# Where TensorE's small results stand in PSUM, and when a weight block's size is taken

## The chip, the cores and the metric

The kernel runs on one core of one Trainium2 chip. The time is the device time of one execution in microseconds (us). Five engines work side by side, each in the order of its own queue: TensorE (PE, matmuls and transposes; its weight loads are shown as PEld), VectorE (DVE), ScalarE (ACT), GpSimd (POOL), and SyncE (SP), which here only issues DMAs. Operands lie in SBUF, results of TensorE in PSUM, which has eight banks of 512 fp32 columns on each of 128 partitions.

## What is computed

Attention with a threshold, for 8 batches of 8 heads with 576 rows of 64, and behind it a feed-forward layer of 512 to 2048 to 512 with a softplus:

```python
scores = scale * np.matmul(q, k.transpose(0, 1, 3, 2))
thresh = np.max(scores, axis=-1, keepdims=True) - tau
scores = np.where(scores >= thresh, scores, -1000000000.0)
scores = scores - np.max(scores, axis=-1, keepdims=True)
attn = np.exp(scores)
attn = attn / (np.sum(attn, axis=-1, keepdims=True) + 1e-09)
attn_out = np.matmul(attn, v)
# (B, H, S, D) to (B * S, H * D), then
h = x @ w_in
g = np.maximum(h, 0.0) + np.log1p(np.exp(-np.abs(h)))
return g @ w_out
```

The weights `w_in` and `w_out` arrive as 64-bit floats. The kernel makes of each a scaled pair of fp16 numbers (a high and a low half), and its larger products are sums of three fp16 products.

## The kernel before

**Tiles and steps.** A unit is one batch and two heads; there are 32 units of 9 tiles of 128 score rows, 288 tiles in all. One pass of the main loop (line 1023) is a step and belongs to tile `g`. The letters of `PAT` (line 36) give the order in which a step issues its work: `R` the row maximum of tile g+2 (`row_max`, DVE, result `negm`), `e` its exponentials (`exps`, ACT, `e_all`, and then `thr`), `m` the mask of tile g+1 (`mask`, DVE, which reads the scores a second time), `h` and `l` the high and low fp16 halves of the weights (POOL, DVE), `T` transposes, `f` a share of the feed-forward matmuls, `p` a point, `S` the scores of tile g+3 (`scores`, PE), `x` the extras of the unit, a second `f`, `v` and `w` (`prep_w`, one block of weights in every second step), and a second `p`. So a step has two points.

**Points.** `defer(n, f)` (line 891) runs `f` at the nth point from now. A chain such as matmul, then copy, then use is spread over points in this way, so that no engine's queue has an instruction at its head whose input isn't there yet. From step 36 on (`TQ`), DVE, ACT and POOL each keep the order in which the program issues (class `Queue`, line 153; in the profile most lines of these engines are therefore L160). Before that, and on PE always, the framework orders instructions by priority and by its own estimate of when they are ready.

**PSUM.** Four of the eight banks are the scores': two buffers `banks[0]` and `banks[1]` (line 475), each of two banks, for the two halves of a tile's 576 columns. A half fills columns 0 to 287 of its bank. Tile n uses `banks[n % 2]`, so the scores of tile n+2 wait for the mask of tile n. The other four banks are a ring of four with the tag `g`. All other results of PE take their turns in it: the transposes of q and k (`tr`), those of the weights in the first five units (`tm`, `tr`; these units are "whole" and work in fp32), the products with v (`pv`), hidden layer (`h`, line 728) and output (`o`, line 792), and the small results that this change is about:
- `top_...` (line 193): one column spread over all partitions by a matmul, 128 columns, read by DVE; 8 times, one for each group of four weight blocks
- `topv` (line 384): the same for v, once in each unit
- `size_...` (line 292): four matmuls that sum a weight block over its columns, 4 columns, copied by ACT into `sums_w`; 32 times
- `rT` (line 629): the transpose of a unit's row sums, 9 partitions of 128 columns, read by ACT, once in each unit

**A block of weights.** `prep_w` (line 276) loads a block of 128 by 512 through `to_f32` (line 209). The 64-bit words are made into a 32-bit float in steps: `first` (ACT, the high word as a magnitude), `clamp` (POOL), and then `second` with n = 0, 1, 2 (DVE): the shift by three bits, the sign put in, and the low word's three bits put in. After the shift, one point on, `size` is taken. When the four blocks of a group are done, `over_all` finds the largest size, and `scaled` and `split` make the fp16 pairs. The blocks start in steps 0, 2, 4 and so on up to 62.

Of the kernel before, what the change touches and what calls it, by code (L numbers as in the profile page):

```python
# [25 lines left out]
P = 128  # L26
NG = 6
TB = 2
SB = 2
# [9 lines left out]
VO = (7, 8, 11, 12)  # L39
RT = 1  # L40
Q9 = (0.9, 1.1, 0.9, 1.1, 1.1, 0.8, 1.2, 0.6, 1.1)
WS2 = 2
LT = 4
WB = 3
NW = 33
# [21 lines left out]
def tile_kernel(ctx: ExitStack, tc: tile.TileContext, q, k, v, tau, w_in, w_out, out):  # L67
# [28 lines left out]
    ps_g = ctx.enter_context(tc.tile_pool(name="ps_g", bufs=GB, space=PSUM))  # L96

    nc.scalar.preload_act_table_set("exp_and_others")

    ones = apool.tile([P, S], F32, tag="R", bufs=1, name="ones")[:, 0:P]  # L100
    make_identity(nc, ones)
# [85 lines left out]
    def over_all(name, cols, then):  # L187

        col = cpool.tile([P, 1], F32, tag="col", bufs=3, name=f"col_{name}")
        vec.reduce_max(col, cols, axis=AX.X, apply_absolute_value=True)  # L190

        def spread():
            ps = ps_g.tile([P, 512], F32, tag="g", name=f"top_{name}")
            nc.tensor.matmul(ps[:, 0:P], col.to_broadcast([P, P]), ident, start=True, stop=True)
            defer(1, lambda: take(ps))

        def take(ps):
            top = cpool.tile([P, 1], F32, tag="top", bufs=3, name=f"top_{name}")
            vec.reduce_max(top, ps[:, 0:P], axis=AX.X)
            then(top)  # L200

        defer(1, spread)
# [6 lines left out]
    def to_f32(src, name, size, then, spare):  # L209

        while reading[0] >= WB or live[0] + 2 > NW:
            force()
        live[0] += 1
        if src.dtype == F32:
            m = piece([P, DM], F32, f"wa_{name}")
            nc.sync.dma_start(m, src)

            def magnitudes():
                a = wpool.tile([P, DM], F32, tag="wi", bufs=WB, name=f"wc_{name}")
                act.activation(a, m, AF.Abs)  # L220
                defer(1, lambda: size(a))
                defer(3, lambda: then(m))

            defer(WD, magnitudes)
            return
        reading[0] += 1
        words = wpool.tile([P, 2 * DM], U32, tag="wi", bufs=WB, name=f"wc_{name}")
        nc.sync.dma_start(words, src.bitcast(U32))
        words = words.rearrange("p (n t) -> p n t", t=2)
        low, high = words[:, :, 0], words[:, :, 1]  # L230

        def first():
            m = piece([P, DM], F32, f"wa_{name}")
            act.activation(m, high.bitcast(F32), AF.Abs, scale=2.0 ** 16)
            defer(1, lambda: clamp(m))

        def clamp(m):
            pool.tensor_scalar(out=m, in0=m, scalar1=W_MAX, scalar2=W_MIN, op0=ALU.min, op1=ALU.max)
            defer(1, lambda: second(m, 0))

        def second(m, n):
            mu = m.bitcast(U32)
            if n == 0:
                i = vec.tensor_scalar(out=mu, in0=mu, scalar1=3, scalar2=None, op0=ALU.logical_shift_left)
                defer(1, lambda: size(m))
            elif n == 1:
                to = piece([P, DM], F32, f"wb_{name}") if spare else m
                i = vec.scalar_tensor_tensor(out=to.bitcast(U32), in0=high, scalar=0x80000000, in1=mu,
                                                   op0=ALU.bitwise_and, op1=ALU.bitwise_or)
                m = to  # L250
            else:
                i = vec.scalar_tensor_tensor(out=mu, in0=low, scalar=29, in1=mu,
                                                   op0=ALU.logical_shift_right, op1=ALU.bitwise_or)
            behind(i, masked)
            if n < 2:
                defer(WS2, lambda: second(m, n + 1))
            else:
                reading[0] -= 1
                defer(1, lambda: then(m))

        defer(WD, first)
# [13 lines left out]

    def prep_w(kind, g, n):

        ms, tops = blocks.setdefault((kind, g), ([], []))
        late = WL.index((kind, g)) >= LATE

        wide = (w_in if kind == "i" else w_out).dtype != F32
        if n == 0:
            tops.append(cpool.tile([P, 16], F32, tag="sums_w", bufs=2, name=f"sums_{kind}{g}"))

        def got(m):
            ms.append(m)
            if n == 3:
                over_all(f"{kind}{g}", tops[0], scaled)

        def add(m):  # L290

            ps = ps_g.tile([P, 512], F32, tag="g", name=f"size_{kind}{g}_{n}")
            high = m.bitcast(BF16).rearrange("p (f t) -> p f t", t=2)[:, :, 1]
            for c in range(4):
                nc.tensor.matmul(ps[:, c:c + 1], high[:, c * P:(c + 1) * P], part, start=True, stop=True)
            defer(1, lambda: act.copy(tops[0][:, 4 * n:4 * n + 4], ps[:, 0:4]))

        def scaled(top):
            scale = cpool.tile([P, 1], F32, tag="wscale", bufs=2, name=f"wscale_{kind}{g}")
            to_scale(scale, top, 8)  # L300
            inverse(p_w[kind][:, g:g + 1], scale)
            for i in range(4):
                defer(2 * i, lambda i=i: split(i, scale))

        def split(i, scale):
            m = ms[i]
            w = piece([P, 2, DM], F16, f"w_{kind}{g}_{i}")
            if late:
                act.activation(w[:, 0, :], m, AF.Copy, scale=scale)
            act.activation(m, m, AF.Copy, scale=scale)  # L310
            defer(1, lambda: split_out(i, m, w))

        def split_out(i, m, w):
            if late:
                pool.tensor_tensor(out=w[:, 1, :], in0=m, in1=w[:, 0, :], op=ALU.subtract)
            else:
                halves(w[:, 0, :], w[:, 1, :], m)
            if kind == "i":
                wi[g, i] = w
            else:  # L320
                wo[4 * g + i] = w
            if i == 3:
                ready.add((kind, g))

        src = w_in[n * P:(n + 1) * P, g * 512:(g + 1) * 512] if kind == "i" else w_out[(4 * g + n) * P:(4 * g + n + 1) * P, :]
        to_f32(src, f"{kind}{g}_{n}", add, got, not late)


# [50 lines left out]
    def top_v(s):  # L379
# [1 line left out]
        vec.tensor_reduce(tops, s.vn.rearrange("p s d -> p (s d)"), axis=AX.X, op=ALU.max, apply_absolute_value=True)  # L381

        def spread():
            ps = ps_g.tile([P, 512], F32, tag="g", name=f"topv_{s.i}")
            nc.tensor.matmul(ps[:, 0:P], tops.to_broadcast([P, P]), ident, start=True, stop=True)
            defer(1, lambda: take(ps))

# [84 lines left out]


    e_all = cpool.tile([P, EB, S], F32, name="e_all")
    banks = [ps_s.tile([P, 2, 512], F32, tag="s", name=f"s_{i}") for i in range(SB)]
    nth = [0]

    def scores(s, t):
# [147 lines left out]
        vec.reciprocal(s.rs, s.rs)  # L626

    def row_scales_T(s):
        ps = ps_g.tile([P, 512], F32, tag="g", name=f"rT_{s.i}")
        nc.tensor.transpose(ps[0:9, 0:P], s.rs, ident)  # L630
        defer(1, lambda: row_scales_out(s, ps))

# [471 lines left out]
```

## Time and profile before

| | us |
|---|---|
| median of three runs | 1297.32 (1296.87 to 1297.4) |
| the profiled execution | 1296.41 |
| its span in the profile | 1294.6 |

The granted clock of TensorE was 0.996 of full speed on average. The profile's lines name an instruction group by its source line, engine, operation and the buffers it writes and reads (`out<-in`), then the count, the busy time, the mean duration in ns, and after the second bar the idle time of the engine just before, with what ended most of it (`<-`). The order of time (the timeline) has the start, the duration, the engine and line, and in square brackets the idle time before it. In the page's slices, each digit is the busy share of a fortieth of the span, in tenths:

```profile
PE   5999988888999999999999999999999999999998
PEld 4655544455565565665566656566657755554455
DVE  6889878988878987888778877786677666640111
ACT  5887887877877777777777787768676767644321
```

### The profile page before, as it was taken

The page shows a single profiled execution, that of the slowest core. Times are in us where ns is not written, and L with a number is a line of the kernel's source. Part 1 is how long each engine was busy: PE and PEld are TensorE (multiplying, and loading weights), DVE is VectorE, ACT ScalarE, POOL GpSimd, SP SyncE. Part 2 cuts the span into 40 slices and gives each one's busy share as a digit, 9 for nine tenths or more (in the row PEclk, how much of TensorE's full clock was granted, in tenths as well). Part 3 has the DMA queues.
Part 4 walks back from the last instruction along what each step waited for, and adds up shares of the span by engine and source line. Part 5 has one row for each costly group of instructions (what it writes and reads, how often), then busy time and mean ns, then how long its engine had stood idle before and what let it go on. Part 6 is the DMA issues. An engine that isn't in the chain of part 4 may idle for free.

```text
span 1294.6 us, 21819 instructions
## 1 busy us (share of the span) xinstructions
PE 1229.4 (95%) x7173; PEld 742.0 (57%) x7173; DVE 931.0 (72%) x1735; ACT 900.4 (70%) x1723; POOL 894.8 (69%) x970
## 2 busy tenths in 40 slices
PE   5999988888999999999999999999999999999998
PEld 4655544455565565665566656566657755554455
DVE  6889878988878987888778877786677666640111
ACT  5887887877877777777777787768676767644321
POOL 2465888888876787678777877787667777564332
PEclk9999989999999999999999999999999999999999
DMA  4545457756776777768766787776557555420010
GB/s 130 160 143 149 121 125 176 173 107 136 176 143 149 137 177 156 150 143 172 151 150 146 168 141 153 144 163 140 131 123 159 122 127 109 98 65 17 1 42 17
DMA packets 368738, 167.92 MB, mean 130 GB/s; under 512 B 320208, under 2 KB 346224, under 8 KB 368624
## 3 DMA queue, kind: packets, MB, share of 16 engines
q1 hardware_dynamic: 368624, 166.52, 58.1%
q8 instruction: 57, 0.93, 0.3%
q14 instruction: 57, 0.47, 0.1%
HBM read 56.62 MB, written 10.63 MB: 52 GB/s over the span
## 4 chain that ended last, share of the span: by engine, by line
PE 36%; ACT 16%; DVE 9%; POOL 8%; issue 7%; DMA 3%; SPq 0%; DVEq 0%; POOLq 0%; ACTq 0%
PE o L792 14%; PE h L728 12%; ACT st L160 5%; PE s L493 5%; ACT L160 5%; POOL g L160 4%; PE pv L608 3%; DVE h L160 3%; DVE e_all L160 2%; ACT e_all L160 2%; DVE negm L160 2%; POOL xl L160 1%; POOL h L160 1%; ACT q L160 1%; ACT kT L160 1%
## 5 line engine op out<-in xcount | busy, mean ns | idle before, releaser
L792 PE MATMUL o<-w_o,g 128*128 128x512 f16 x1728 | 405.0, 380 | 2.1 <-DVE xp L160 1.2
L728 PE MATMUL h<-xh,w_i 128*128 128x512 f16 (+1 forms) x1280 | 361.7, 359 | 5.9 <-ACT sums_i L160 3.6
L160 POOL TENSOR_SCALAR h<-e_all 128x576 f16<-128x576 f32 x243 | 228.9, 945 | 112.9 <-DVE e_all L160 110.4
L160 ACT ACTIVATE e_all<-s,negm 128x576 f32<-128x576 f32 x288 | 213.6, 742 | 119.1 <-DVE negm L160 113.1
L728 PEld LDWEIGHTS <-w_i 128*128 128x128 f16 x1920 | 179.0, 98 | 168.7 <-issue 13.2
L160 DVE SCALAR_TENSOR_TENSOR e_all<-s,thr,e_all 128x576 f32<-128x576 f32 x288 | 232.8, 808 | 53.9 <-ACT thr L160 53.1
L160 DVE TENSOR_REDUCE negm<-s 128x1 f32<-128x576 f32 x288 | 215.1, 747 | 69.6 <-PE s L493 68.2
L792 PEld LDWEIGHTS <-g 128*128 128x128 f16 x1728 | 159.2, 98 | 174.2 <-issue 3.5
L160 DVE SCALAR_TENSOR_TENSOR h<-e_all,h 128x576 f16<-128x576 f32 x243 | 236.5, 973 | 19.0 <-POOL h L160 18.5
L728 PE MATMUL h<-xl,w_i 128*128 128x512 f16 (+1 forms) x640 | 230.3, 360 | 1.2 <-POOL xl L160 1.1
L160 POOL TENSOR_SCALAR g<-st 128x512 f16<-128x512 f32 x144 | 97.7, 678 | 165.0 <-ACT st L160 160.2
L160 DVE SCALAR_TENSOR_TENSOR acc<-o,c,acc 128x512 f32<-128x512 f32 x108 | 80.1, 742 | 154.5 <-PE o L792 154.1
L160 POOL TENSOR_TENSOR g<-st,g 128x512 f16<-128x512 f32 x144 | 172.2, 1196 | 12.0
L493 PE MATMUL s<-kT,q 128*128 128x288 f32 x768 | 152.9, 327 | 15.5 <-DVE e_all L160 12.5
L160 ACT ACT_TABLE_LOAD x119 | 152.7, 1283 | 3.6 <-DVE negm L160 1.4
L160 ACT ACTIVATE st<-h,c 128x512 f32<-128x512 f32 x144 | 91.1, 683 | 79.6 <-PE h L728 78.8
L493 PEld LDWEIGHTS s<-kT,q 128*128 128x128 f32 x768 | 114.7, 191 | 51.7 <-DVE e_all L160 37.6
L608 PE MATMUL pv<-eT,vt 128*128 128x288 f16 x972 | 139.7, 287 | 3.3 <-DVE xp L160 2.5
L493 PE MATMUL s<-kT,qT 128*128 128x288 f32 x512 | 106.4, 329 | 4.0 <-DVE e_all L160 3.5
L608 PEld LDWEIGHTS <-vt 128*128 128x128 f16 x972 | 88.8, 98 | 37.4 <-issue 4.9
L160 ACT COPY xp<-pv 64x288 f32<-64x288 f32 (+3 forms) x133 | 50.5, 383 | 78.2 <-PE pv L608 74.4
L160 ACT ACTIVATE st<-st,c 128x512 f32<-128x512 f32 x144 | 96.2, 715 | 2.3
(118 smaller groups left out, 1497.9 us busy)
## 6 DMA issues: line engine op xcount, KB each, us to landing
q<-q SPq DMA_DIRECT2D x62, 192.0 KB
kn<-in_k_dram SPq DMA_DIRECT2D x32, 256.0 KB
qn<-in_q_dram SPq DMA_DIRECT2D x32, 256.0 KB
vn<-in_v_dram SPq DMA_DIRECT2D x32, 256.0 KB
wc_i<-in_moe_w_in_dram SPq DMA_DIRECT2D x16, 512.0 KB
wc_o<-in_moe_w_out_dram SPq DMA_DIRECT2D x16, 512.0 KB
qT<-qT SPq DMA_DIRECT2D x62, 128.0 KB
out_dram<-acc SPq DMA_DIRECT2D x14, 512.0 KB
```

Source lines behind the costliest of these rows:

```text
L160: i = getattr(self.eng, name)(*args, **kwargs)
L493: nc.tensor.matmul(sp[:, hf, 0:HS], lhs, s.kT[j][:, hf * HS:(hf + 1) * HS], start=(m == 0), stop=(m == len(parts) - 1))
L608: nc.tensor.matmul(o[:, 0:HS], s.vt[:, a, :], s.eT[j][:, b, x0:x0 + HS], start=(n == 0), stop=(n == 2 * NC))
L728: nc.tensor.matmul(bank[:, i * u.T:(i + 1) * u.T], wi[g, cc][:, a, e], x[cc], start=(cc == 0 and m == 0), stop=(cc == NCC - 1 and m == 2))
L792: nc.tensor.matmul(o, u.g[fc][m // 2][:, sl], wo[fc][:, m % 2, :], start=(n == 0), stop=(n == 3 * QF - 1))
```

## The change

The two buffers of the scores are made at the start of the kernel, and four pieces of 224 columns are named in them: the columns behind the scores in each of the four banks.

```diff
+    banks = [ps_s.tile([P, 2, 512], F32, tag="s", name=f"s_{i}") for i in range(SB)]
+    beside = [banks[i // 2][:, i % 2, S // 2:] for i in range(4)]
```

The four small results go there, and no longer into the ring: `topv` into the first bank of `banks[0]`, `top` into its second, `rT` into the first bank of `banks[1]`, and the sizes into its second.

```diff
-            ps = ps_g.tile([P, 512], F32, tag="g", name=f"top_{name}")
+            ps = beside[1]
...
-            ps = ps_g.tile([P, 512], F32, tag="g", name=f"topv_{s.i}")
+            ps = beside[0]
...
-        ps = ps_g.tile([P, 512], F32, tag="g", name=f"rT_{s.i}")
+        ps = beside[2]
```

The sixteen sizes of a group of blocks stay in PSUM, in sixteen columns of their own (two sets by turns), and DVE takes their maximum there. ACT's copies into `sums_w` are gone.

```diff
+        sums = beside[3][:, 16 * (WL.index((kind, g)) % 2):][:, 0:16]
...
-            ps = ps_g.tile([P, 512], F32, tag="g", name=f"size_{kind}{g}_{n}")
             for c in range(4):
-                nc.tensor.matmul(ps[:, c:c + 1], high[:, c * P:(c + 1) * P], part, start=True, stop=True)
-            defer(1, lambda: act.copy(tops[0][:, 4 * n:4 * n + 4], ps[:, 0:4]))
+                nc.tensor.matmul(sums[:, 4 * n + c:4 * n + c + 1], high[:, c * P:(c + 1) * P], part, start=True, stop=True)
```

The steps of a block are put in another order: after the shift the low bits, one point on; then its size, two points after that (`SZ`); then its sign, three points after the low bits. The sum of points from the shift to the end of the block is five, as before. The size reads the upper 16 bits of each word, which the low bits don't change.

```diff
             if n == 0:
                 i = vec.tensor_scalar(out=mu, in0=mu, scalar1=3, scalar2=None, op0=ALU.logical_shift_left)
-                defer(1, lambda: size(m))
             elif n == 1:
+                i = vec.scalar_tensor_tensor(out=mu, in0=low, scalar=29, in1=mu,
+                                                   op0=ALU.logical_shift_right, op1=ALU.bitwise_or)
+                defer(SZ, lambda: size(m))
+            else:
                 to = piece([P, DM], F32, f"wb_{name}") if spare else m
                 i = vec.scalar_tensor_tensor(out=to.bitcast(U32), in0=high, scalar=0x80000000, in1=mu,
                                                    op0=ALU.bitwise_and, op1=ALU.bitwise_or)
                 m = to
-            else:
-                i = vec.scalar_tensor_tensor(out=mu, in0=low, scalar=29, in1=mu,
-                                                   op0=ALU.logical_shift_right, op1=ALU.bitwise_or)
             behind(i, masked)
             if n < 2:
-                defer(WS2, lambda: second(m, n + 1))
+                defer(1 if n == 0 else 3, lambda: second(m, n + 1))
```

More of the change, by code (lines that the diff above doesn't have):

```diff
@@ L41 @@
 Q9 = (0.9, 1.1, 0.9, 1.1, 1.1, 0.8, 1.2, 0.6, 1.1)
-WS2 = 2
+SZ = 2
 LT = 4
@@ L276, in prep_w @@
     def prep_w(kind, g, n):
-        ms, tops = blocks.setdefault((kind, g), ([], []))
+        ms = blocks.setdefault((kind, g), [])
         late = WL.index((kind, g)) >= LATE
-        wide = (w_in if kind == "i" else w_out).dtype != F32
-        if n == 0:
-            tops.append(cpool.tile([P, 16], F32, tag="sums_w", bufs=2, name=f"sums_{kind}{g}"))
+        sums = beside[3][:, 16 * (WL.index((kind, g)) % 2):][:, 0:16]
         def got(m):
@@ L287, in got @@
             if n == 3:
-                over_all(f"{kind}{g}", tops[0], scaled)
+                over_all(f"{kind}{g}", sums, scaled)
         def add(m):
-            ps = ps_g.tile([P, 512], F32, tag="g", name=f"size_{kind}{g}_{n}")
             high = m.bitcast(BF16).rearrange("p (f t) -> p f t", t=2)[:, :, 1]
             for c in range(4):
-                nc.tensor.matmul(ps[:, c:c + 1], high[:, c * P:(c + 1) * P], part, start=True, stop=True)
-            defer(1, lambda: act.copy(tops[0][:, 4 * n:4 * n + 4], ps[:, 0:4]))
+                nc.tensor.matmul(sums[:, 4 * n + c:4 * n + c + 1], high[:, c * P:(c + 1) * P], part, start=True, stop=True)
         def scaled(top):
@@ L474, in tile_kernel @@
     e_all = cpool.tile([P, EB, S], F32, name="e_all")
-    banks = [ps_s.tile([P, 2, 512], F32, tag="s", name=f"s_{i}") for i in range(SB)]
     nth = [0]
```

## The prediction

> **What bounds the kernel now.** I read the page's busy shares first, then a table by stage, then the groups of instructions for what TensorE (PE) waits for, and last the order of time around single waits.
>
> ```profile
> PE 1229.4 (95%) x7173; PEld 742.0 (57%) x7173; DVE 931.0 (72%) x1735; ACT 900.4 (70%) x1723; POOL 894.8 (69%) x970
> ```
>
> ```profile
> 30.00:130.00 100.00, 92.66 (x577) 59.97 (x577) 88.61 (x175) 81.14 (x223) 55.24 (x62) 1.00 0.51 147
> 130.00:230.00 100.00, 86.59 (x499) 50.06 (x497) 85.19 (x159) 82.54 (x174) 84.13 (x84) 0.97 0.58 142
> 230.00:330.00 100.00, 87.49 (x506) 50.88 (x507) 91.29 (x165) 73.91 (x139) 85.02 (x86) 1.00 0.64 143
> 430.00:1030.00 600.00, 591.93 (x3532) 366.94 (x3531) 473.67 (x879) 443.66 (x805) 453.47 (x493) 1.00 0.71 149
> ```
>
> The columns of the table are the stretch, its length, then busy time of PE, its weight loads, DVE, ACT and POOL. PE sets the time: 1229.4 of 1294.6 us. From 430 to 1030 us it idles 600 - 591.93 = 8.1 us in all, so nothing worth having is left there. From 30 to 330 us it idles 7.3 + 13.4 + 12.5 = 33.3 us, and DVE is then as full as PE (88.6, 85.2, 91.3 of 100 us). In that stretch the 32 blocks of the MoE weights are prepared. So the change can win only before 330 us, and there DVE stands close behind PE.
>
> **What the small results cost now.** PE's idle time, by what it ran next and what ended the wait:
>
> ```profile
> L728 PE MATMUL h<-xh,w_i 128*128 128x512 f16 (+1 forms) x1280 | 361.7, 359 | 5.9 <-ACT sums_i L160 3.6 <-ACT q L160 1.9 <-DVE xp L160 0.2
> L433 PE MATMUL tr<-identr,k 128*128 128x128 f32 x256 | 37.0, 260 | 8.6 <-DVE k L160 6.6 <-ACT rt L160 1.3 <-DVE top_o L160 0.6
> L530 PE MATMUL tm<-identr,e_all 128*128 128x128 f32 x180 | 29.5, 288 | 0.9 <-ACT sums_o L160 0.5 <-DVE topv L160 0.4
> L385 PE MATMUL topv<-identr,vtop 128*128 128x128 f32 x64 | 12.9, 283 | 2.4 <-DVE xp L160 2.4
> L295 PE MATMUL size_i<-part,wa_i 128*128 128x1 bf16 x64 | 4.0, 167 | 1.3 <-ACT gw L160 0.8 <-DVE wa_i L160 0.5
> L295 PE MATMUL size_o<-part,wa_o 128*128 128x1 bf16 x64 | 4.0, 167 | 8.2 <-DVE wa_o L160 7.6 <-DVE xp L160 0.6
> L194 PE MATMUL top_i<-identr,col_i 128*128 128x128 f32 x8 | 1.6, 286 | 0.5 <-ACT sums_i L160 0.5
> ```
>
> Two kinds of wait are in these rows. In the first, `size` waits for DVE's words of its block: 0.5 + 7.6 = 8.1 us. In the second, a matmul waits for one of the four `g` banks, because a small result holds it or because the small result needs one: 3.6 + 1.3 + 0.6 + 0.5 + 0.4 + 2.4 + 0.8 + 0.6 + 0.5 = 10.7 us. Together 18.8 us; that is all that the change can take away directly.
>
> **The `size` waits are worth little.** One of them, and what follows:
>
> ```profile
> 250.69 0.25 PE L295 MATMUL size_o<-part,wa_o 128*128 128x1 bf16 x4 [1.15 <-DVE wa_o L160]
> ...
> 251.88 0.80 DVE L160 SCALAR_TENSOR_TENSOR e_all<-s,thr,e_all 128x576 f32<-128x576 f32 x1
> ...
> 252.75 0.43 PEld L493 LDWEIGHTS s<-kT,q 128*128 128x128 f32 x3 [0.44 <-DVE e_all L160]
> ```
>
> PE loses 1.15 us at `size`, and 2 us later the next scores wait anyway, for the mask that frees their bank (251.88 + 0.80 = 252.68, scores at 252.75). Take the first wait away and PE only reaches the second one sooner, since the mask stands behind the same block work in DVE's queue. In the change `size` comes two points after the DVE operation it reads, not one, so these 8.1 us go, but I keep only 1 (bounds 0 and 8.1).
>
> **The bank waits are worth more.** The longest:
>
> ```profile
> 189.12 0.65 ACT L160 ACTIVATE wa_i<-wc_i 128x512 f32<-128x512 f32 x1
> 189.25 0.82 DVE L160 SCALAR_TENSOR_TENSOR e_all<-s,thr,e_all 128x576 f32<-128x576 f32 x1 [2.04 <-ACT thr L160]
> 189.67 0.15 ACT L160 COPY sums_i<-size_i 128x4 f32<-128x4 f32 x1
> ...
> 189.87 0.59 PE L728 MATMUL h<-xh,w_i 128*128 128x512 f16 x1 [3.64 <-ACT sums_i L160]
> ...
> 193.73 0.77 PE L493 MATMUL s<-kT,qT 128*128 128x288 f32 x4
> ```
>
> A hidden-layer matmul waits 3.64 us for the bank of a `size`, until ACT, busy with other things, copies four columns. Here the mask was over at 190.07 and the scores came at 193.73, so nothing else would have held PE: 3.6 us are won. The granted clock (the column after PE's busy time in this table of PE alone) fell with the stall and stayed low after it:
>
> ```profile
> 186.00:190.00 4.00, 0.36 (x4) 0.53 0.39 77
> 190.00:193.40 3.40, 3.40 (x10) 0.55 0.18 43
> 193.40:197.00 3.60, 3.60 (x26) 1.00 0.86 173
> ```
>
> So some 1.5 us of slow matmuls (3.4 us at 0.55) go with it; I count them as nothing, since the mask would hold the scores from 190.07 on. I take 4 of the remaining 7.1 us (bounds 0 and 7.1), because some of those waits are again followed by scores that wait for their mask.
> Gain: 1 + 3.6 + 4 = **8.6 us** (bounds 0 and 18.8).
>
> **What else goes or is exchanged.** The 32 copies of `sums` (2.5 + 2.5 us of ACT, as 16 of 158 and 16 of 157 ns) leave ACT's queue. ACT has 19 us idle between 30 and 130 us, so they count as nothing; at most 5 us if ACT set the end.
>
> ```profile
> L160 ACT COPY sums_i<-size_i 128x4 f32<-128x4 f32 x16 | 2.5, 158 | 0.6 <-PE size_i L295 0.6
> L160 ACT COPY sums_o<-size_o 128x4 f32<-128x4 f32 x16 | 2.5, 157 | 1.1 <-PE size_o L295 1.1
> ```
>
> DVE's three operations on a block are the same three in another order: nothing. No matmul is removed, and none is lengthened. The block is ready at the same point as before (1 + 3 + 1 points after the shift, against 2 + 2 + 1), so its buffers and DMAs keep their places.
>
> **What is added: waits by bank.** The columns are free, but the banks are not: the scores of tile n stand in `banks[n % 2]`. No row of before shows two tenants in one bank, so I must assume how they are kept apart. If only by address, nothing is added. If by bank, each small result is ordered against every reader and writer of the scores in that bank. The Trainium skill's page "PSUM — Partial Sum Buffer", section "PSUM bank collisions raise a hardware error", says that engines must be kept apart by bank and group of 32 partitions, reads included, whatever the columns; it speaks against the change, and by it the costs below exist, while by addresses alone the sum would be the gain of 8.6 us.
>
> a) `size`, 32 times, in `banks[1]`. Block i is started in step 2i; its `size` now stands at the second point of step 2i + 4, just after the scores of tile 2i + 7 (odd, same bank) and the second share of that step's other PE work. The row maximum of that tile must now wait for it:
>
> ```profile
> 67.20 0.77 PE L493 MATMUL s<-kT,q 128*128 128x288 f32 x4
> ...
> 67.90 1.83 PE L562 MATMUL pv<-gw,vn 128*64 128x320 f32 x6
> 68.01 0.76 DVE L160 TENSOR_REDUCE negm<-s 128x1 f32<-128x576 f32 x1
> ...
> 69.66 0.66 PE L530 MATMUL tm<-identr,e_all 128*128 128x128 f32 x4
> ```
>
> Here DVE takes the maximum at 68.01, 0.04 us after the scores end (67.97); the second point is where the transposes `tm` begin, 69.66; with the 0.25 us of `size` the maximum would start 1.9 us late. DVE idles 11.4 us in the 100 us of that stage, some 0.7 per two tiles (about 32 tiles), so up to 1.2 us of it could reach PE, 19 times before tile 45: 0 to 23 us. Below zero is excluded, since a wait alone shortens nothing. Before tile 36 DVE's order is not chained by hand, and the mask of the tile before can go first; after 130 us DVE mostly arrives late. I take 3.5.
>
> b) The spreads of `topv` and `top` (32 and 8), in `banks[0]`, read by DVE. In about every second unit the scores just before them are an even tile's, so PE must wait for that tile's exponential and DVE, with its next maximum queued behind, for PE:
>
> ```profile
> 383.45 0.39 PE L385 MATMUL topv<-identr,vtop 128*128 128x128 f32 x2
> ...
> 383.88 0.29 DVE L160 TENSOR_REDUCE topv<-topv 128x1 f32<-128x128 f32 x1 [0.89 <-PE topv L385]
> ...
> 384.46 0.75 DVE L160 TENSOR_REDUCE negm<-s 128x1 f32<-128x576 f32 x1
> ...
> 385.05 0.74 ACT L160 ACTIVATE e_all<-s,negm 128x576 f32<-128x576 f32 x1
> ```
>
> The exponential ends at 385.79, so the spread and everything behind it on DVE come 2.3 us later, about 16 times: 0 to 37 us.
>
> c) `rT`, 32 times, in `banks[1]`, read by ACT. In every second unit it follows an odd tile's scores:
>
> ```profile
> 606.19 0.27 PE L630 MATMUL rT<-identr,rs 128*9 128x128 f32 x1
> ...
> 606.39 0.76 DVE L160 TENSOR_REDUCE negm<-s 128x1 f32<-128x576 f32 x1 [0.39 <-PE s L493]
> ...
> 608.62 0.25 ACT L160 ACTIVATE rt<-rT 9x128 f32<-9x128 f32 x1
> ```
>
> If the maximum must follow ACT's read, it starts 608.87 - 606.39 = 2.5 us late, at most 16 times: 0 to 40 us.
> What covers b and c: most of them fall after 330 us, where DVE is often that late already and PE goes on with other matmuls:
>
> ```profile
> 922.92 0.88 PE L493 MATMUL s<-kT,qT 128*128 128x288 f32 x4
> ...
> 927.40 0.75 DVE L160 TENSOR_REDUCE negm<-s 128x1 f32<-128x576 f32 x1
> ```
>
> Here the maximum begins 3.6 us after the scores end, in a stretch where PE is idle 1.3% of the time. I take 0.5 us for each, 1 in all; without that cover, several us each.
>
> **Sum.** 1294.6 - 8.6 + 3.5 + 1 = 1290.5 us of span. The profiled execution took 1296.41 us, 1.8 more than its span, so 1292.3; the median of the three runs shown is 0.9 above it: **1293 us**, 0.3% faster.
>
> **Rivals.** (1) The bank waits land on DVE's path, and it ends slower. Mechanism: in the stage of the whole tiles DVE takes each maximum as soon as the scores end, so an added wait goes through maximum and mask to the scores two tiles on. Half of a's upper end is 11; b and c, past their cover, some 1 us in each seventh of 72 events, 10; less the gain: 1297.3 - 8.6 + 21 = 1310 us. It decides as soon as DVE reaches the maximum within 0.1 us of the scores' end and has no mask to do first. For it: DVE's 85 to 91%. Against it: the 3.6 us lags that cost PE nothing.
> (2) It does nothing that counts: the time won before each score matmul is waited off at the next mask, as at 252.75, and the small costs eat the rest: 1297 us. For it: DVE's share, above all between 230 and 330 us.
> (3) All 18.8 us are won and the waits cost nothing: 1297.3 - 18.8 = 1278.5 us. Against it: the scores' waits for their masks.
>
> **Chances.** Forecast (1286 to 1294) 0.34, rival 1 0.34, rival 2 0.23, rival 3 0.09. Rival 2 reaches a little over the upper edge of the bound of 0.2% (2.6 us, about what a measurement of this kernel can tell from no change). Faster by more: 0.43; within: 0.20; slower: 0.37. The range is 1283 to 1311: it leaves out most of rival 3 and the upper part of rival 1. The forecast's own range is 1286 to 1296.
>
> **What would show it.** Right: no PE wait on `sums`, none at `size`, the 3.64 us wait and its like gone, PE's idle time before 330 us down from 33.3 to about 28. For rival 1: DVE's waits before `negm` for PE grow, on `size` above all, and DVE waits before `topv`; PE's waits of `s` on `e_all` grow by more than the gain. For rival 2: these grow by just the gain. The forecast is wrong if PE's own order, made anew around the waits, moves hidden-layer matmuls enough to change the stage after 430 us, which no row here can tell.

## The result and the profile after

| | us |
|---|---|
| before | 1297.36, median of 4 (1296.87 to 1297.58) |
| after | 1318.16, median of 4 (1315.59 to 1319.26) |
| ratio | 1.0158 (95% interval 1.0143 to 1.0173) |
| span of the profiled execution after | 1315.7 |

The change makes the kernel 21 us slower. The forecast was 1293 us with a range to 1311: the sign is wrong, and the time lies 7 us above the range.

The page's busy shares of after:

```profile
PE 1246.8 (95%) x7173; PEld 747.8 (57%) x7173; DVE 925.2 (70%) x1735; ACT 899.8 (68%) x1691; POOL 891.7 (68%) x970
```

The same 7173 matmuls now keep PE busy for 1246.8 us, against 1229.4. The instructions are the same, so it isn't work that was added. The table by stage (stretch, length, busy time of PE, weight loads, DVE, ACT, POOL, then the granted clock, DMA share and GB/s):

```profile
30.00:130.00 100.00, 94.74 (x583) 60.46 (x581) 87.63 (x177) 80.99 (x211) 55.53 (x62) 1.00 0.52 147
130.00:230.00 100.00, 85.87 (x470) 49.83 (x468) 81.37 (x147) 75.59 (x152) 76.21 (x77) 0.93 0.54 130
230.00:330.00 100.00, 87.03 (x486) 50.16 (x487) 87.71 (x166) 75.72 (x134) 81.98 (x84) 0.95 0.67 135
430.00:1030.00 600.00, 588.83 (x3446) 358.27 (x3444) 466.08 (x865) 440.82 (x798) 448.96 (x492) 1.00 0.74 148
```

Three things are to be seen against the rows of before. From 130 to 330 us PE issues 956 matmuls where it issued 1005, and POOL and DVE are less busy, too. The clock, 0.97 and 1.00 there before, is 0.93 and 0.95. And the stage from 430 to 1030 us, in which I had found nothing to win, has something to lose: 3446 matmuls in place of 3532 in the same 600 us.

What the change was to take away is gone. These groups are PE's at the hidden layer and at the sizes (L296); since the small results are now pieces of the scores' banks, their output is named `s`:

```profile
L727 PE MATMUL h<-xh,w_i 128*128 128x512 f16 (+1 forms) x1280 | 363.3, 360 | 4.7 <-ACT q L164 2.2 <-DVE xp L164 1.8 <-POOL xh L164 0.5
...
L296 PE MATMUL s<-part,wa_o 128*128 128x1 bf16 x64 | 4.5, 170 | 0.0
```

No matmul waits for `sums` any more, and none waits at a size: the 8.2 us ahead of `size_o` became 0.0. What came in their place stands in the list of DVE's waits (what waited, for what, us in all, times, longest):

```profile
DVE negm L164 <- ACT rt L164: 28.4, 15, 3.6
...
DVE topv L164 <- PE s L385: 23.4, 7, 4.0
...
DVE topv L164 <- PE s L492: 16.9, 12, 2.4
DVE negm L164 <- PE s L296: 16.4, 18, 3.4
```

A row maximum `negm` reads the scores. It needs nothing from `rt` (the row sums, copied out by ACT) nor from a size. That it waits 28.4 us for the one and 16.4 us for the other can only come from the shared bank. So tenants of one bank are kept apart by bank, and not by address, which the rows of before left open; the Trainium skill's page "PSUM — Partial Sum Buffer", section "PSUM bank collisions raise a hardware error", asks for just that, and the trace agrees (28.4 us in 15 waits between instructions that touch different columns).

Where the 21 us arise is seen by taking the start of each tile's scores in the trace after, less the start of the same tile's scores before (us, worked out from the two traces):

```
tile    36    48    60    72    96   156   192   228   264
after  2.1   5.4   8.9   9.0   9.6  14.0  16.7  19.7  19.5
```

There are two losses. **One of 9 us** has come by tile 72, while the weights are prepared. **Another of some 11 us** comes behind it, in even steps: from tile 72 to 228, 10.7 us in 156 tiles, which are 4.33 times 36 tiles, so 2.5 us in every four units (36 tiles). I took the two apart.

### The profile page after: what moved, and what is told of

It is laid out like the page before. It is cut to its first block, busy times and chain, and to the rows that moved or that the text cites. A ratio compares the mean times of both kernels' runs of the same rounds, so it can differ in the third digit from the quotient of the medians.

```text
span 1315.7 us, 21755 instructions
## 1 busy us (share of the span) xinstructions
PE 1246.8 (95%) x7173; PEld 747.8 (57%) x7173; DVE 925.2 (70%) x1735; ACT 899.8 (68%) x1691; POOL 891.7 (68%) x970
## 4 chain that ended last, share of the span: by engine, by line
PE 50%; ACT 17%; DVE 13%; POOL 8%; issue 8%; DMA 3%; SPq 0%; ACTq 0%; POOLq 0%; DVEq 0%
PE h L727 16%; PE o L791 15%; PE s L492 8%; ACT st L164 5%; ACT L164 5%; PE pv L607 4%; POOL g L164 4%; DVE negm L164 4%; ACT e_all L164 3%; PE pv L561 3%; DVE e_all L164 3%; DVE h L164 2%; POOL h L164 2%; DVE wa_o L164 1%; PE tr L433 1%
## 5 line engine op out<-in xcount | busy, mean ns | idle before, releaser
L791 PE MATMUL o<-w_o,g 128*128 128x512 f16 x1728 | 410.4, 382 | 1.3 <-ACT kT L164 0.4
L164 DVE SCALAR_TENSOR_TENSOR e_all<-s,thr,e_all 128x576 f32<-128x576 f32 x288 | 232.6, 809 | 46.4 <-ACT thr L164 44.4
L164 DVE SCALAR_TENSOR_TENSOR h<-e_all,h 128x576 f16<-128x576 f32 x243 | 230.8, 950 | 11.5 <-POOL h L164 10.7
L164 POOL TENSOR_SCALAR g<-st 128x512 f16<-128x512 f32 x144 | 94.6, 657 | 168.8 <-ACT st L164 166.8
L492 PE MATMUL s<-kT,q 128*128 128x288 f32 x768 | 154.1, 330 | 16.3 <-DVE e_all L164 13.5
```

The source lines that it names most:

```text
L164: i = getattr(self.eng, name)(*args, **kwargs)
L492: nc.tensor.matmul(sp[:, hf, 0:HS], lhs, s.kT[j][:, hf * HS:(hf + 1) * HS], start=(m == 0), stop=(m == len(parts) - 1))
L791: nc.tensor.matmul(o, u.g[fc][m // 2][:, sl], wo[fc][:, m % 2, :], start=(n == 0), stop=(n == 3 * QF - 1))
```

## The experiments

All times are medians; a ratio is to the kernel before on the same chip, with its 95% interval, and can differ by up to 0.001 from the quotient of the two medians. "Ring" is the four `g` banks, "in the banks" the free columns beside the scores. The theories are told in the expectations, which stood before each run. Each experiment is also read by the table of starts, less those of before:

```
tile                        36    48    60    72    96   156   192   228   264
order only                 3.1   4.8   6.7   9.1   8.8   9.0   9.0   9.1   9.0
place only                 2.6   1.0   1.0   3.0   3.6   8.0  10.6  13.7  13.5
after, topv in the ring    0.7   2.2   4.4   4.4   5.7   6.8   7.7   8.6   9.1
after, rT in the ring      1.8   6.3   7.6   7.0   7.6  11.2  13.0  15.3  14.6
after, both in the ring   -0.5   2.3   2.5   4.1   4.5   4.6   4.5   4.5   4.5
low bits first, even      -0.8  -1.6  -1.8   0.6   0.9   0.9   0.8   0.9   0.8
old order, bunched         3.3   7.6   8.3  10.6   8.8   8.8   8.7   8.8   8.8
place only, free bank      6.1   4.5   5.3   6.9   7.0   7.6   8.1   8.9   9.3
sizes and top in banks    -0.2  -0.4  -0.7   1.7   2.2   2.4   2.5   2.5   2.5
after, sizes in the ring   7.5  12.0  12.4  15.4  16.7  21.1  23.7  26.6  26.4
after, banks exchanged     9.1  12.4  17.4  17.7  19.0  23.5  26.1  29.1  29.0
even, banks exchanged      3.0   2.3   3.4   4.1   3.4   3.6   3.6   3.7   3.7
```

### The order of a block's steps alone

The kernel before, with the new order and its distances of 1 and 3 points; all small results stay in the ring.

```diff
             if n == 0:
...
-                defer(1, lambda: size(m))
             elif n == 1:
+                i = vec.scalar_tensor_tensor(out=mu, in0=low, scalar=29, in1=mu,
...
+                defer(SZ, lambda: size(m))
+            else:
                 to = piece([P, DM], F32, f"wb_{name}") if spare else m
...
-                defer(WS2, lambda: second(m, n + 1))
+                defer(1 if n == 0 else 3, lambda: second(m, n + 1))
```

> The kernel before with the new order of a block's steps alone (low bits, size two points later, sign), all small results in the ring. Theory A (the loss comes from waits that keep engines apart in the scores' banks): no bank is shared, so no loss, and the waits of size for DVE's words shrink; 1291 to 1298 us. Rival B (the new order of the steps is at fault, as it moves DVE's work against the maxima): 1307 us or more. Rival C (any change makes PE's order anew and moves the time by some per cent): anywhere between 1285 and 1315, with no wait to show for it.

Measured: 1305.27 us, 1.0061 (1.0040 to 1.0082), above what I expected and a little below rival B's 1307. The whole loss has come by tile 72 (9.1 us), and behind it the difference stays at 9.0. No small result shares a bank with scores here, so this loss isn't one of banks.

### The places alone

After, with the old order and its distances of 2 and 2.

```diff
-SZ = 2
+WS2 = 2
...
-                defer(1 if n == 0 else 3, lambda: second(m, n + 1))
+                defer(WS2, lambda: second(m, n + 1))
```

> The changed kernel with the old order of a block's steps; all four small results stay in the scores' banks. Theory A: most of the loss stays, 1308 to 1318 us; a size then comes at the second point of an odd step, where its bank's maximum has been taken, so the maxima's waits for size (16.4 us in the changed kernel) nearly go, while those for topv and rT stay. Rival B: 1295 to 1301 us.

Measured: 1312.21 us, 1.0116 (1.0094 to 1.0138). It is the mirror image: 3.0 us at tile 72, then a steady rise to 13.5 at tile 264.

### `topv` or `rT` back in the ring

After, with one of the two back in the ring; and then with both.

```diff
-            ps = beside[0]
+            ps = ps_g.tile([P, 512], F32, tag="g", name=f"topv_{s.i}")
...
-        ps = beside[2]
+        ps = ps_g.tile([P, 512], F32, tag="g", name=f"rT_{s.i}")
```

> The changed kernel with topv alone back in the ring. Theory A: in the changed trace the scores fall back by 2.0 us around tiles 132 to 136 of each 36 tiles, where topv waits for an exponential; 5.7 such periods lie behind tile 72, and there are a few more before, so 1304 to 1310 us, and DVE's waits before topv fall from 40 us to under 20. Rival B: no change, 1316 to 1320. Rival C: no relation to the period of 36 tiles.

> The changed kernel with rT alone back in the ring. Theory A: the step of 0.85 us behind tile 121 of each 36 tiles goes, and the maxima's waits for ACT's read of rT (28.4 us) vanish: 4.8 us behind tile 72 and some before, 1309 to 1315 us. Rival B: no change, 1316 to 1320.

> The changed kernel with both topv and rT back in the ring; sizes and top stay in the scores' banks, the gaps of 1 and 3 points stay. Theory A with D: the fall-back behind tile 72 goes entirely (difference of the scores' starts to before flat from tile 72 to 264 within 1 us), and what is left is the bunching of e1, less what the sizes' place gives back: 1299 to 1304 us. If topv's and rT's costs don't add up: 1306 or more.

Measured: with `topv` back 1306.63 us, 1.0071 (1.0053 to 1.0088); with `rT` back 1311.80, 1.0115 (1.0096 to 1.0135); with both 1300.95, 1.0027 (1.0015 to 1.0038). These are as expected, but that DVE's waits before `topv` fall to 21.2 us, and not under 20, with `topv` back. Against the 1.0158 of after these are 0.0087, 0.0043 and 0.0131 less, or 11.3, 5.6 and 17.0 us of 1297 (some 5 of the 17.0 arise by tile 72, 9.0 against 4.1 in the table). The two effects add up (11.3 + 5.6 = 16.9), and with both back the table is flat behind tile 72. So these two results make the second loss, all of it, and `topv` the larger part; from tile 72 to 228 `topv` alone takes (15.3 - 7.0) / 4.33 = 1.9 us in four units, `rT` alone (8.6 - 4.4) / 4.33 = 1.0. How they do it is seen in the order of time of after. First `rT`, in the unit that starts with tile 117 (columns: start, duration, engine and line, operation; idle time before it in brackets):

```profile
481.97 1.41 PE L492 MATMUL s<-kT,q 128*128 128x288 f32 x8
...
483.06 1.27 ACT L164 ACTIVATE st<-h,c 128x512 f32<-128x512 f32 x2
483.22 0.28 PE L629 MATMUL s<-identr,rs 128*9 128x128 f32 x1
...
485.60 0.25 ACT L164 ACTIVATE rt<-s 9x128 f32<-9x128 f32 x1
...
485.88 0.76 DVE L164 TENSOR_REDUCE negm<-s 128x1 f32<-128x576 f32 x1 [3.23 <-ACT rt L164]
486.55 0.81 DVE L164 SCALAR_TENSOR_TENSOR e_all<-s,thr,e_all 128x576 f32<-128x576 f32 x1
...
487.42 0.58 PEld L492 LDWEIGHTS s<-kT,qT 128*128 128x128 f32 x4 [0.29 <-DVE e_all L164]
487.42 0.81 PE L492 MATMUL s<-kT,qT 128*128 128x288 f32 x4
```

The scores of tile 121 end at 483.38. Their maximum could start there, but `rT` (L629) has been put into the same bank, and its reader on ACT stands behind the `st` activations of the feed-forward layer. DVE idles 3.23 us. The mask of tile 120 is the next in DVE's queue; it ends at 487.36, and the scores of tile 122, whose bank it frees, start 0.06 us later. Only their weight load shows a wait for the mask, of 0.29 us, and the matmuls themselves none; yet against before the scores of tile 121 are 11.40 us late (481.97 against 470.57) and those of tile 122 13.31 (487.42 against 474.11). Most of these 1.9 us isn't lost. Thirteen matmuls (nine of `pv`, four of `tr`) that stood behind the scores of tile 122 in before stand ahead of them in after, because PE's order is made anew in each kernel; the scores of tile 123 are 11.84 us late. What stays is 0.4 us at tile 123 and 0.8 at tile 127. The lag against before, tile by tile, around this event and the next:

```
tile    114   119   121   122   123   127   131   133   134   141
after  11.0  11.7  11.4  13.3  11.8  12.2  12.2  11.9  13.8  13.7
```

Then `topv`, at tile 132:

```profile
525.23 0.88 PE L492 MATMUL s<-kT,qT 128*128 128x288 f32 x4
...
529.91 0.89 PE L492 MATMUL s<-kT,qT 128*128 128x288 f32 x4
...
531.66 0.74 ACT L164 ACTIVATE e_all<-s,negm 128x576 f32<-128x576 f32 x1
...
532.45 0.49 PE L385 MATMUL s<-identr,vtop 128*128 128x128 f32 x2
532.98 0.29 DVE L164 TENSOR_REDUCE topv<-s 128x1 f32<-128x128 f32 x1 [3.38 <-PE s L385]
...
534.23 0.81 DVE L164 SCALAR_TENSOR_TENSOR e_all<-s,thr,e_all 128x576 f32<-128x576 f32 x1
...
535.10 0.79 PE L492 MATMUL s<-kT,qT 128*128 128x288 f32 x4
```

The spread of v's maximum (L385) has to wait until ACT has read tile 132's scores for its exponential, which ends at 532.40, 6.3 us after the scores of tile 132 did. DVE's `topv` waits for it 3.38 us, and with it the maximum of tile 133, ready since 530.80, and the mask of tile 132 behind that. Again the next scores, those of tile 134, start 0.06 us after the mask's end (535.04). PE's order differs here too: the spread stood ahead of the scores of tile 133 in before and stands behind them in after, and six output matmuls and three transposes more stand ahead of those of tile 134. Here most of the delay stays, 1.7 us from tile 133 to tile 141 (11.93 to 13.66). This is the step of my prediction under b, where it stands with 2.3 us an event; what I had wrong is that other work covers it.

So the second loss comes with these two results in the banks, but by which way isn't separated. From tile 110 on, PE's matmuls stand in exactly the order of before in every kernel that keeps `topv` and `rT` in the ring. With `rT` in the banks 110 of 4931 places differ, with `topv` 216, with both 341. Each kernel that has the waits has a changed order as well, and no run has the one without the other.

### Is it the bunching of DVE's work?

The new order puts the shift and the low bits one point apart and the sign three points later. A step has two points, and blocks start in every second step. So the sign of one block, the shift of the next and its low bits all fall into one step, and the next step has none; the old order had one and two. To try this apart from the order: the first kernel with even distances (low bits first, but 2 and 2, and the size one point after the low bits), and the kernel before with its old order but distances of 4 and 1.

```diff
-SZ = 2
+SZ = 1
...
-                defer(1 if n == 0 else 3, lambda: second(m, n + 1))
+                defer(2, lambda: second(m, n + 1))
```

```diff
-                defer(WS2, lambda: second(m, n + 1))
+                defer(4 if n == 0 else 1, lambda: second(m, n + 1))
```

> As e1 (new order of the steps, all small results in the ring), but shift, low bits and sign two points apart each, as the old order had them, and the size one point after the low bits. Theory D (the 9 us of e1 come from bunching: with gaps of 1 and 3 points all three DVE operations of the blocks, some 3 us, fall into the odd steps, and the masks there come late): the loss goes, 1293 to 1299 us, and PE's waits of s on e_all before 300 us fall from 16 us to about 6 to 9. Rival E (the sign, written in place, waits for the size's matmuls): that wait stays in e7, and so do several us of the loss, 1301 or more. Rival F (low bits ahead of the sign cost DVE time by themselves): 1305.

> The kernel before with its old order of the steps, but with gaps of 4 and 1 points in place of 2 and 2, so that shift, sign and low bits all fall into the odd steps; the size stays where it was, and the block is ready at the next point. Theory D: the loss of e1 comes without the new order, 1302 to 1308 us. Rivals E and F: no loss, 1296 to 1299.

Measured: the new order spread evenly 1297.61 us, 1.0002 (0.9993 to 1.0011), the same as before; the old order bunched 1304.78, 1.0061 (1.0046 to 1.0076), the same loss as the new order with 1 and 3. The loss goes with the bunching and not with the order. One step of each, at the same tiles, DVE's operations on a block being those of 128x512 (left out: the low halves of the attention weights, which are 128x576, and small results). First the order alone, bunched:

```profile
193.58 0.82 DVE L160 SCALAR_TENSOR_TENSOR e_all<-s,thr,e_all 128x576 f32<-128x576 f32 x1 [2.28 <-ACT thr L160]
...
195.33 1.09 DVE L160 SCALAR_TENSOR_TENSOR wa_i<-wc_i,wa_i 128x512 uint32<-128x512 uint32 x1
196.34 1.37 DVE L160 TENSOR_SCALAR wa_i<-wa_i 128x512 uint32<-128x512 uint32 x1
...
198.74 1.23 DVE L160 SCALAR_TENSOR_TENSOR wa_i<-wc_i,wa_i 128x512 uint32<-128x512 uint32 x1
199.90 0.74 DVE L160 TENSOR_REDUCE negm<-s 128x1 f32<-128x576 f32 x1
200.56 0.80 DVE L160 SCALAR_TENSOR_TENSOR e_all<-s,thr,e_all 128x576 f32<-128x576 f32 x1
...
201.43 0.79 PE L493 MATMUL s<-kT,qT 128*128 128x288 f32 x4 [1.72 <-DVE e_all L160]
```

And the same step with even distances:

```profile
187.15 0.82 DVE L160 SCALAR_TENSOR_TENSOR e_all<-s,thr,e_all 128x576 f32<-128x576 f32 x1 [2.00 <-ACT thr L160]
...
188.90 1.09 DVE L160 SCALAR_TENSOR_TENSOR wa_i<-wc_i,wa_i 128x512 uint32<-128x512 uint32 x1
189.91 1.37 DVE L160 TENSOR_SCALAR wa_i<-wa_i 128x512 uint32<-128x512 uint32 x1
...
192.31 0.75 DVE L160 TENSOR_REDUCE negm<-s 128x1 f32<-128x576 f32 x1
192.98 0.81 DVE L160 SCALAR_TENSOR_TENSOR e_all<-s,thr,e_all 128x576 f32<-128x576 f32 x1
...
193.85 0.80 PE L493 MATMUL s<-kT,qT 128*128 128x288 f32 x4 [0.33 <-DVE e_all L160]
194.38 1.15 DVE L160 SCALAR_TENSOR_TENSOR wa_i<-wc_i,wa_i 128x512 uint32<-128x512 uint32 x1
```

The third operation on a block stands before the maximum in the one (198.74) and behind the mask in the other (194.38). From mask to mask it is 200.56 - 193.58 = 6.98 us against 5.83, and the wait of PE's scores for the mask is 1.72 us against 0.33. In the next step, which has no operation on a block in the bunched kernel, DVE makes up 0.7 of these 1.15 us (the masks behind start at 202.99 and 196.12). PE doesn't: from the scores of tile 52 to those of tile 54 it runs the same matmuls in both kernels, in 12.02 us against 10.07. Both have a stretch at half clock in this time (stretch, length, PE's busy time, clock, DMA share, GB/s; the bunched kernel, then the even one):

```profile
202.60:206.00 3.40, 3.40 (x10) 0.50 0.39 87
...
189.80:193.20 3.40, 3.40 (x11) 0.50 0.66 162
```

The stretches are of the same length, so the 1.95 us between the two kernels aren't the clock's here. But the wait of 0.33 us is short in part because PE comes to it late: its slow stretch lies ahead of the wait, that of the bunched kernel behind it.

Over the whole stage the clock is a second way from the bunching to the time, next to the late masks. PE's waits of scores for masks between 30 and 300 us are 16.2 us in the order alone, 14.1 in the old order bunched, 9.7 with even distances and 6.2 in the kernel before. The stretches at half clock between 40 us and the scores of tile 96 sum to 23.9, 20.5, 13.7 and 6.8 us in the same order. A matmul of 512 columns comes every 0.427 us in them and every 0.216 us otherwise, so they cost at most half their length: the 17.1 and 13.7 us more of the bunched kernels can be worth up to 8.5 and 6.8 of the 8.8 us that both have lost by tile 96. Their length alone doesn't set the loss, since even distances have 6.8 us more than before and lose 0.9. The bunching is shown as the cause; how much of the loss goes through the masks and how much through the clock is not. (The old order bunched also has each block ready one point later, six points after the shift.)

### The bank that the next scores overwrite

The places alone, but `topv` and `rT` go into the bank of the tile whose mask is the next thing to be over, and no longer into a fixed one.

```diff
-            ps = beside[0]
+            ps = banks[nth[0] % SB][:, 0, S // 2:]
...
-        ps = beside[2]
+        ps = banks[nth[0] % SB][:, 0, S // 2:]
```

> As e2 (old order of the steps, small results in the scores' banks), but topv and rT each go to the bank that the next scores will overwrite, and not always to the same one. Theory A: topv then needs no exponential that is still to come, and no maximum waits for ACT's read of rT; the steady fall-back of e2 (2.3 us in each 36 tiles, 13 us in all behind tile 72) shrinks to under 0.5 per 36 tiles, 1298 to 1303 us. If it is only that a small result of any kind shares a bank, or ACT's and DVE's reads of it, whatever the moment: 1308 to 1313 as e2.

Measured: 1307.66 us, 1.0078 (1.0062 to 1.0095). The rise behind tile 72 falls from 10.5 us (3.0 to 13.5) to 2.4 (6.9 to 9.3), as expected; the total is above the expected range, because 6.9 us are lost by tile 72 and some 3.5 more from tile 264 to 272, behind the end of the table (places alone 2.9 there, after 1.6). DVE's groups of this kernel for the maximum and the mask:

```profile
L164 DVE SCALAR_TENSOR_TENSOR e_all<-s,thr,e_all 128x576 f32<-128x576 f32 x288 | 232.7, 808 | 65.2 <-ACT thr L164 36.6 <-ACT rt L164 18.2 <-PE s L296 9.1
...
L164 DVE TENSOR_REDUCE negm<-s 128x1 f32<-128x576 f32 x288 | 215.0, 746 | 66.5 <-PE s L492 65.2
```

The wait of the maximum for `rt` is gone; it now stands before the mask (18.2 us), partly in place of the mask's wait for its threshold (`thr`, 44.4 us with the fixed banks, 36.6 here). So a wait for a bank is not priced by its length: behind tile 72 columns in the scores' banks cost little here. That it is because the mask waits for something else at that time anyway is argued: only 7.8 of the 18.2 us replace another wait, and PE's order is changed less, too (75 of 4931 places from tile 110 on, against 341).

### The sizes

After with the sizes back in the ring, and their copies with them; after with the banks of sizes and `top` exchanged, so that the sizes stand beside the even tiles; the kernel before with only sizes and `top` in the banks; and, with low bits first and even distances, sizes and `top` in exchanged banks (in these last two `topv` and `rT` are in the ring).

```diff
-        sums = beside[3][:, 16 * (WL.index((kind, g)) % 2):][:, 0:16]
...
+            ps = ps_g.tile([P, 512], F32, tag="g", name=f"size_{kind}{g}_{n}")
...
+            defer(1, lambda: act.copy(tops[0][:, 4 * n:4 * n + 4], ps[:, 0:4]))
```

```diff
-            ps = beside[1]
+            ps = beside[3]
...
-        sums = beside[3][:, 16 * (WL.index((kind, g)) % 2):][:, 0:16]
+        sums = beside[1][:, 16 * (WL.index((kind, g)) % 2):][:, 0:16]
```

> The changed kernel with the sizes alone back in the ring (and copied by ACT), the new order of the steps kept. Theory A with D: the maxima's waits for size (16.4 us of DVE) go, but the bunched DVE work stays and sets the same masks late, so little is won: 1313 to 1318 us. If the waits for size were the main cost of the stage with the weights, as the forecast's rival had it: 1306 to 1311.

> The changed kernel with the banks of size and top exchanged: a size then stands in the bank of the tile whose maximum is already taken. Theory A: the maxima's waits for size (16.4 us of DVE in the changed kernel) go, the masks wait instead but have more slack; 1311 to 1317 us, little, since e2 and e8 show that the bunched DVE work sets the same masks late anyway. If these waits are a cost of their own: 1304 to 1310.

> The kernel before with sizes and top alone in the scores' banks; topv and rT in the ring, old order of the steps and its gaps. Theory A: nothing behind tile 72; before it the ring is freed of 40 small results and ACT of 32 copies, as e5 against the changed kernel says that the sizes' place by itself gives several us back; 1290 to 1297 us. If any sharing of a bank costs: 1299 to 1303.

> As e10, but with the low bits first at even gaps (as e7), and the size, which then comes in even steps, in the bank whose maximum is already taken. Theory A with D: like e10 or some us better, as size no longer waits for DVE's words; 1289 to 1297 us. If low bits first makes the sign wait for size: 1298 or more.

Measured: with the sizes back in the ring 1324.44 us, 1.0207 (1.0189 to 1.0226), 0.0049 or 6 us more than after; banks exchanged 1328.50, 1.0245 (1.0220 to 1.0270), 0.0087 or 11 us more; only sizes and `top` in the banks 1299.06, 1.0019 (1.0010 to 1.0028); even distances with banks exchanged 1300.17, 1.0020 (1.0011 to 1.0029). All four missed what I expected: the first two are slower than any of the theories had them, the last two lie in the ranges of their rivals. Two things follow. With the old order, sizes and `top` in the banks cost 2.5 us (0.0019 of 1297), and with low bits first and even distances 2.3 (1.0020 against 1.0002): the gain that the forecast counted on from the ring isn't there even without the rest. With the bunched order they win: after with `topv` and `rT` in the ring is at 1.0027, the order alone, with everything in the ring, at 1.0061. So the same move costs some 2.5 us or wins some 4, by the order around it.

For the exchanged banks, DVE's waits for sizes:

```profile
DVE e_all L164 <- PE s L296: 13.1, 9, 3.3
```

In after the maximum waited for sizes (16.4 us); here the mask does (13.1 us), and `topv` (4.8). A mask frees the bank of the next scores, a maximum doesn't at once, and that may be why waits of about the same length in all cost 11 us more. That is an argument and not shown: with even distances, and the size one point earlier, the same exchange does no such harm. In the stage of the weights the effects don't add up. PE's order is made anew in each kernel there, and DVE is about as full as PE. The 6 us of the sizes in the ring, and the 6.9 us by tile 72 in the free-bank kernel against 3.0 with fixed banks, have no cause that these runs settle.

None of these kernels is faster than the kernel before.

## Why the prediction was wrong

**The balance.** From the ratios: the order with its distances costs 0.0061 (7.9 us); sizes and `top` in the banks, on top of it, give back 0.0061 - 0.0027 = 0.0034 (4.4); `topv` and `rT` in the banks cost 0.0158 - 0.0027 = 0.0131 (17.0). Sum: 20.5 us. Each term is uncertain by some 3 us, and they depend on what else is changed: with the old order of the steps `topv` and `rT` cost 0.0116 - 0.0019 = 0.0097 (12.6).

**The gain (8.6 us): its steps came, its worth did not.** In after the waits for `sums` and at the sizes are gone, with the stall of 3.64 us. But PE's idle time from 30 to 330 us, which was to fall from 33.3 to about 28 us, is 32.4 (300 less the 94.74, 85.87 and 87.03 us of the table). The time won was waited off at the masks, as rival 2 had it. PE's waits of scores for masks between 30 and 300 us, in the kernel before and in the one with only sizes and `top` in the banks:

```profile
PE s L493 <- DVE e_all L160: 6.2, 12, 1.1
```

```profile
PE s L492 <- DVE e_all L164: 10.4, 16, 1.5
```

They grow by 4.2 us, and that kernel is no faster than before. It tests the 7.6 us counted for the waits on the ring, and not the 1 us for the sizes: with the old order these still wait for DVE's words, 6.5 us for `w_out` (the row below) and 2.1 for `w_in`, against 8.1 in all before.

```profile
PE s L296 <- DVE wa_o L164: 6.5, 7, 1.7
```

The rule I applied at 252.75, that the time won at a size is lost at the next mask, I should have applied to the 3.64 us too: one event where the mask was early said little about what comes behind it.

**"DVE's three operations on a block are the same three in another order: nothing."** This step failed first: 7.9 us. I summed points (1 + 3 + 1 against 2 + 2 + 1) to see that a block is ready at the same time, and never looked at which step each operation falls into. The two kernels of the bunching test separate the two ideas: new order without bunching 1.0002, bunching without the new order 1.0061. The data for it stood in the prediction: DVE was 85 to 91% full in that stage, so a step with one operation more (1.1 to 1.4 us in the rows above) runs past its end.

**a) Sizes: 3.5 us taken, 0 to 23 the bounds.** The mechanism was right: maxima wait for sizes, 18 times, 16.4 us in all. Its price isn't those 16.4 us but +2.5 or -4.4 us, with the gain of the sizes in it, by the order around it. The exclusion of values below zero was right for a wait alone, but not for what could be measured, the move as a whole.

**b and c) `topv` and `rT`: 1 us taken, 17.0 measured.** This is the largest error, and it is the cover that failed, not the waits behind it, which came. DVE's waits before `topv` are 23.4 + 16.9 = 40.3 us in 19 (rows above), and those for `rt`, 28.4 us, are new. Before:

```profile
DVE topv L160 <- PE topv L385: 19.5, 17, 2.8
```

I had looked at one tile whose maximum began 3.6 us late without harm and took it for the stage. Whether such a lag is harmless depends on the tile: where the mask behind it ends just before the scores that need its bank (0.06 us at tiles 122 and 134), the delay is passed on, 0.8 us by tile 127 and 1.7 by tile 141. Most events are covered, as I had argued, and a few decide: of the 19 waits before `topv`, seven, about one in four units, are on the spread itself and take 23.4 us (3.3 each), and four units lose 1.9 us by `topv`, about what stays of the one event at tile 132 (1.7 us). A mean over all events hides these, and my 0.5 us in all for each of b and c lies below even one of them by `topv`.

**Rival 1 named the place**, DVE's path from maximum to mask to scores. It gave 1310 us, since it priced b and c at 10 us where they cost 17, counted 11 for a, and did not know the bunching. Of its marks, longer waits before `topv` and `negm` came; "on `size` above all" did not hold, as `rt` (28.4) and `topv` (20.8 more than before) are the larger. That PE's waits of scores for masks would grow by more than the gain was a poor mark: they are 24.5 us against 16.1 in the whole span, 8.4 more, while the loss is 21. The sign that I had named last came as well: PE's order changed in the stage after 430 us. Around the waits of b and c products with v, transposes, output matmuls and five hidden-layer matmuls in every 36 tiles stand at other places, and with `topv` and `rT` in the ring the order is that of before and the stage loses nothing.

## What to carry over

Free columns are not a free bank: before a small result goes beside a live tile, write down who reads that tile, who stands behind the new wait in each queue, and how much time the tightest tile, not the typical one, has between that queue and PE. When a step is moved, add up the work per step of the engine that it runs on, not only the time until the chain's end. Before a delay is put down to a wait, see whether PE's order is still the same. And time won ahead of a wait that remains is not won, which has to be checked for each gain and not for one of them.

## What the hardware showed that I had not expected

**The clock falls for less than I thought.** These are PE's windows in after (stretch, length, busy time, clock, DMA share, GB/s), each pair the 3.4 us ahead of a slow stretch and the stretch itself:

```profile
146.80:150.20 3.40, 1.30 (x9) 1.00 0.44 145
150.20:157.00 6.80, 6.29 (x25) 0.50 0.36 98
187.80:191.20 3.40, 0.70 (x5) 0.99 0.92 205
191.20:194.60 3.40, 3.40 (x13) 0.51 0.54 123
```

PE was not idle for a whole 3.4 us ahead of them, only mostly: it was busy 1.30 and 0.70 of 3.40 us (0.92 to 1.54 ahead of the other three), with no single gap over 2.7 us, and then ran at half clock for 3.4 or 6.8 us. After has five such stretches ahead of its tail (23.9 us), before has one (6.8 us). So stalls of 2 us can cost more than themselves wherever PE is then the bound; the bunching test above has what that can be worth. A rule isn't to be had from it either: ahead of the one stretch of before PE was busy for 2.31 us.

```profile
182.80:186.20 3.40, 2.31 (x16) 1.00 0.75 240
```

The Trainium skill's page "TensorE: Matmul & The Clock Gate", section "Why this matters for your kernels", advises no idle gaps over some 3 us; by that alone no stretch of after should have slowed here, and the trace differs (largest gap 2.70 us).

**PE's idle time understates the loss.** From 430 to 1030 us PE idles 11.2 us against 8.1, 3.1 more, but tiles 108 to 252, which lie in that stretch, fall back by 8.3 us (11.0 to 19.3). From the scores of tile 108 to those of tile 144 the same 776 matmuls take 137.06 us in after and 134.38 before; of these 2.7 us, 1.1 are shown as idle. Two rows of after's order of time:

```profile
483.33 0.38 PE L727 MATMUL h<-xh,w_i 128*128 128x512 f16 x1
...
483.76 0.59 PE L727 MATMUL h<-xh,w_i 128*128 128x512 f16 x2
```

A matmul of the hidden layer lasts 0.38 us alone and 0.59 us as two in a row: the second adds 0.21. A gap of up to 0.17 us between two of them is therefore not seen as idle at all. That this is where the rest hides is my reading and wasn't tried.
